# Local attention and an FFN in one kernel: seven wide chunks in place of twelve narrow ones, and a longer attention lead

## The chip, the cores and the metric

The kernel runs on one core of one Trainium2 chip. The metric is the time on the device in microseconds, from start to end of one execution; below are three runs and one profiled execution of the kernel before. A core has five engines with a queue each, worked off in order: TensorE (PE; its weight loads are PEld), VectorE (DVE), ScalarE (ACT), GpSimd (POOL) and SyncE (SP), which here only issues DMAs.

## The reference

```python
def _attn_ref(q, k, v, n_global, n_local):         # q, k, v: 4 batches, 8 heads, 768 tokens, 64 dims
    scores = scale * np.matmul(q, k.transpose(0, 1, 3, 2))
    is_global = pos[None, :] < int(n_global)       # 8
    is_local = (rel >= 0) & (rel < int(n_local))   # 96; rel = query position - key position
    dist = np.where(is_global & ~is_local, float(n_local), np.abs(rel))
    scores = np.where(is_global | is_local, scores - slopes * dist, -1e9)
    a = np.exp(scores - np.max(scores, axis=-1, keepdims=True))
    a = a / (np.sum(a, axis=-1, keepdims=True) + 1e-09)
    return np.matmul(a, v)

def _moe_ref(x, w_in, w_out):                      # 3072 x 512, 512 x 2048, 2048 x 512
    h = x @ w_in
    return np.maximum(0.01 * h, h) @ w_out
```

The attention's output, laid out as 3072 tokens by 512, is the FFN's input. The weights come in as float64, the rest as float32.

## The kernel before

**Attention.** A step is a block of 128 queries of one batch (24 steps), and each step has four units of two heads. A query block needs at most two blocks of keys, its own and one that holds the 32 first keys and the 96 before the block; the first step of a batch needs its own alone. `scores` multiplies queries by keys, VectorE adds the bias and takes the row minimum (line 199), ScalarE the exponential (209). `normalise` follows one unit later, `transposes` two, `attn_v` three. Units of the first batch (24, "plain") use float32 products, of two instructions each; the other 72 ("split") use pairs of rounded parts. The first eight units ("lead") run before the FFN. In these, `normalise` makes a diagonal matrix of the row factors on VectorE (line 223), and a float32 product with it transposes and scales in one (242); in all others Pool scales the probabilities (225) and TensorE transposes them (244). In the first six units, two products that nothing reads follow the transposes (`warm`, line 232).

**Weights.** 32 pieces of 512 KB of float64 bits, 16 for each matrix, in the order in which hidden tiles need them. `load_piece` brings one into a buffer of the pool `big` (ten buffers for several uses), and is called for piece p + 2 once piece p's conversion has been written down. `split_float64` converts with one step on ScalarE (436), three on VectorE (437, 439, 441), a rounding on Pool or ScalarE and a subtraction on Pool (449). Six pieces are converted during the lead.

**FFN.** A chunk is 256 tokens, twelve in all. A slot is one hidden tile of 128 units for one chunk: `hidden` makes twelve products into one PSUM tile (lines 639 to 641: 4 blocks of the input by 3 pairs of rounded parts), and four steps on ScalarE and VectorE apply the activation and split the result (643 to 648); `project` adds three products per token block of 128 to the chunk's output sums (655 to 657), one slot later. The first three chunks take the first ten hidden tiles in turn and then the other six, so their output sums are left once in the tile `part` and added to later (366, 369). Attention units and pieces of weights are dealt out evenly over slots. A scheduler orders the instructions of all this on each engine; the queues run them in that order. PSUM has eight banks: six in `ps_x` for hidden tiles, scores, transposes and values in rotation, and two in `ps_o` for output sums.

## Time and profile before

| | |
|---|---|
| runs, us | 738.5, 738.68, 744.76 (median 738.68) |
| span of the profiled execution | 743.0 us, 14545 instructions |
| busy share of the span | PE 97%, PEld 86%, DVE 69%, ACT 56%, POOL 43% |
| DMA | 47.69 MB, 64 GB/s over the span |
| chain that ended last | PE 82%, DVE 11%, issue 2%, DMA 2% |

Of the three runs, the profiled execution's span fits the longest only: 744.76 us holds a span of 743.0 us, the other two are shorter than it. A row of the timeline gives start, duration, engine, line, operation, what is written and read, shapes and a count. A matmul's duration includes its way through the array, so that products overlap in it; what one costs in a stream is read from the difference of two starts. A row of a group gives busy time and mean duration in ns, and then the engine's idle time before the group, with what ended it. In `64*128 64x256`, 64 is the number of rows of the array, 128 that of its columns, and 256 the columns that stream through.

### The profile page before, as it was taken

Reading aid. Unit: us, or ns where it says so; the run is one execution under the profiler, and the core shown is the slowest. Engines: PE = TensorE matmul, PEld = TensorE weight load, DVE = VectorE, ACT = ScalarE, POOL = GpSimd, SP = SyncE. Lnnn points to the kernel's source line nnn. Section 1 sums busy time; section 2 is a strip of 40 time slices with the busy share of each in tenths; the row PEclk is TensorE's granted clock in tenths of the full one; section 3 lists DMA queues with packets and bytes.
Section 4 is the critical chain, followed back from the end, with each engine's and each line's share of the span. In section 5 each row is a group of like instructions: output and inputs, shape, how many; then the busy total and the mean of one; then the engine's idle time right before and its main releaser. Section 6 shows DMA issues by size and latency. Waiting matters only on the chain.

```text
span 743.0 us, 14545 instructions
## 1 busy us (share of the span) xinstructions
PE 718.6 (97%) x4691; PEld 638.3 (86%) x4691; DVE 515.8 (69%) x1536; ACT 412.7 (56%) x1228; POOL 316.1 (43%) x563
## 2 busy tenths in 40 slices
PE   8979889999999999999999999999999999999995
PEld 7657667788999999999899999999999999999994
DVE  7699999764578877765777677776767776653222
ACT  4545667543566556654666665565656665643321
POOL 3389775831234444445344344445344544300000
PEclk9998999999999999999999999999999999999998
DMA  6454525130012111211211211211101211000000
GB/s 173 148 219 165 166 72 163 58 115 1 22 64 72 57 45 43 71 30 50 69 40 33 69 44 30 72 44 55 61 30 43 72 37 37 33 1 1 29 1 33
DMA packets 38916, 47.69 MB, mean 64 GB/s; under 512 B 5552, under 2 KB 27056, under 8 KB 38832
## 3 DMA queue, kind: packets, MB, share of 16 engines
q1 hardware_dynamic: 38832, 46.69, 20.1%
q8 instruction: 39, 0.64, 0.4%
q14 instruction: 45, 0.37, 0.2%
HBM read 40.37 MB, written 6.29 MB: 63 GB/s over the span
## 4 chain that ended last, share of the span: by engine, by line
PE 82%; DVE 11%; issue 2%; DMA 2%; ACT 1%; POOL 1%; SPq 0%; POOLq 0%; ACTq 0%; DVEq 0%
PE ps_h L641 11%; PE ps_h L640 11%; PE ps_h L639 11%; PE ps_o L655 11%; PE ps_o L656 11%; PE ps_o L657 11%; PE ps_av L287 4%; PE ps_tr L244 4%; DVE w L439 3%; PE ps_sc L191 2%; DVE w L441 2%; PE ps_sc L190 2%; PE ps_sc L188 2%; DVE w L437 1%; DVE gl L648 1%
## 5 line engine op out<-in xcount | busy, mean ns | idle before, releaser
L639 PE MATMUL ps_h<-xh,wih 128*128 128x256 f32 x768 | 219.7, 287 | 0.3 <-DVE xl L280 0.3
L640 PE MATMUL ps_h<-xl,wih 128*128 128x256 f32 x768 | 216.9, 283 | 1.9 <-DVE xl L280 1.9
L641 PE MATMUL ps_h<-xh,wil 128*128 128x256 f32 x768 | 217.1, 283 | 0.9 <-POOL wil L449 0.9
L655 PE MATMUL ps_o<-woh,gh 128*128 128x512 f32 x384 | 158.2, 412 | 1.2 <-ACT gh L647 1.2
L656 PE MATMUL ps_o<-wol,gh 128*128 128x512 f32 x384 | 153.3, 399 | 0.0
L639 PEld LDWEIGHTS ps_h<-xh,wih 128*128 128x128 f32 x768 | 145.9, 190 | 8.3 <-issue 1.2
L640 PEld LDWEIGHTS ps_h<-xl,wih 128*128 128x128 f32 x768 | 146.1, 190 | 7.8 <-DVE xl L280 2.1
L641 PEld LDWEIGHTS ps_h<-xh,wil 128*128 128x128 f32 x768 | 145.9, 190 | 6.9 <-POOL wil L449 1.6
L657 PE MATMUL ps_o<-woh,gl 128*128 128x512 f32 x384 | 142.1, 397 | 5.5 <-DVE gl L648 5.5
L225 POOL TENSOR_SCALAR pr<-pr,rs 128x256 f32<-128x256 f32 (+1 forms) x176 | 97.6, 564 | 106.5 <-DVE rs L218 88.4
L643 ACT ACTIVATE t<-ps_h 128x256 f32<-128x256 f32 x192 | 72.9, 380 | 102.3 <-PE ps_h L641 98.0
L648 DVE TENSOR_TENSOR gl<-t,gh 128x256 fp32r<-128x256 f32 x192 | 89.0, 464 | 52.3 <-ACT gh L647 50.5
L647 ACT CAST gh<-t 128x256 fp32r<-128x256 f32 x192 | 77.2, 402 | 74.7 <-DVE t L644 62.0
L644 DVE TENSOR_TENSOR t<-ps_h,t 128x256 f32<-128x256 f32 x192 | 80.6, 420 | 48.9 <-ACT t L643 46.6
L209 ACT ACTIVATE pr<-pr,nmall 128x256 f32<-128x256 f32 (+1 forms) x192 | 94.0, 490 | 19.2 <-DVE nmall L199 16.9
L55 POOL TENSOR_SCALAR qh<-qkr 128x256 fp32r<-128x256 f32 x72 | 29.9, 416 | 148.5 <-PE ps_sc L190 147.5
L657 PEld LDWEIGHTS ps_o<-woh,gl 128*128 128x128 f32 x384 | 70.0, 189 | 23.1 <-DVE gl L648 7.0
L655 PEld LDWEIGHTS ps_o<-woh,gh 128*128 128x128 f32 x384 | 73.0, 190 | 11.9 <-ACT gh L647 2.1
L656 PEld LDWEIGHTS ps_o<-wol,gh 128*128 128x128 f32 x384 | 72.9, 190 | 8.0
L199 DVE CUSTOM_DVE_ANT_0 pr<-ps_sc,nbw 128x256 f32<-128x256 f32 x96 | 38.9, 418 | 32.3 <-PE ps_sc L191 25.9
L165 ACT CAST kw<-qkr 64x256 fp32r<-64x256 f32 x72 | 29.2, 406 | 55.8 <-DMA qkr<-in_qk_dram 55.6
L166 DVE TENSOR_TENSOR kw<-qkr,kw 64x256 fp32r<-64x256 f32 x72 | 34.2, 476 | 34.4 <-ACT kw L165 33.7
(94 smaller groups left out, 1155.5 us busy)
## 6 DMA issues: line engine op xcount, KB each, us to landing
qkr<-in_qk_dram SPq DMA_DIRECT2D x72, 128.0 KB, 2.5
wst<-in_wi_dram SPq DMA_DIRECT2D x16, 512.0 KB, 4.3
wst<-in_wo_dram SPq DMA_DIRECT2D x16, 512.0 KB, 4.6
vr<-in_vp_dram SPq DMA_DIRECT2D x96, 64.0 KB, 1.9
out_dram<-part SPq DMA_DIRECT2D x24, 256.0 KB, 2.1
qkr<-in_qk_dram SPq DMA_DIRECT2D x72, 64.0 KB, 2.3
kr<-in_qk_dram SPq DMA_DIRECT2D x24, 64.0 KB, 2.6
qr<-in_qk_dram SPq DMA_DIRECT2D x16, 64.0 KB, 2.6
```

The costliest lines, as they stand in the source:

```text
L209: nc.scalar.activation(out=pr[:, j, :n], in_=pr[:, j, :n], func=AF.Exp, scale=-1.0, bias=nm[:, j:j + 1], accum_out=sm[:, j:j + 1])
L225: nc.gpsimd.tensor_scalar(out=pr[:, j, :n], in0=pr[:, j, :n], scalar1=rs[:, j:j + 1], scalar2=1.0, op0=ALU.mult, op1=ALU.mult)
L639: nc.tensor.matmul(ps, lhsT=wih[:, k, fs], rhs=xh[:, k, :], start=(k == 0), stop=False)
L640: nc.tensor.matmul(ps, lhsT=wih[:, k, fs], rhs=xl[:, k, :], start=False, stop=False)
L641: nc.tensor.matmul(ps, lhsT=wil[:, k, fs], rhs=xh[:, k, :], start=False, stop=(k == NK - 1))
L643: nc.scalar.activation(out=t, in_=ps, func=AF.Copy, scale=0.01)
L644: nc.vector.tensor_tensor(out=t, in0=ps, in1=t, op=ALU.max)
L647: nc.scalar.copy(out=gh, in_=t)
L648: nc.vector.tensor_tensor(out=gl, in0=t, in1=gh.bitcast(F32), op=ALU.subtract)
L655: nc.tensor.matmul(o, lhsT=gh[:, ts_], rhs=woh[:, f, :], start=first, stop=False)
L656: nc.tensor.matmul(o, lhsT=gh[:, ts_], rhs=wol[:, f, :], start=False, stop=False)
L657: nc.tensor.matmul(o, lhsT=gl[:, ts_], rhs=woh[:, f, :], start=False, stop=last)
```

## The change

- The FFN has seven chunks of 4, 2, 3, 4, 4, 4 and 3 steps (256 to 512 tokens), each through all 16 hidden tiles, so that there are no partial sums. `ps_o` has four banks and `ps_x` four. A chunk's attention units are dealt out over the first 14 slots of the chunk before.
- The lead has 16 units (four steps). All plain units transpose as the others do, after Pool has scaled the probabilities; the diagonal products and the products that nothing reads are gone, but for five at the very start.
- A plain unit's two heads lie in two halves of the partitions (arrays `qp` and `kp`), so that its two score products stand in different rows of the array and go to two PSUM tiles, of `ps_o` in the lead.
- The pool `big` is gone. Weight pieces have two buffers, which the output tiles take over later; the converted words share three with parts of attention; a chunk's inputs have two pairs.
- Six pieces are converted in the lead, after its steps 5, 7, ... 15, and the other 26 in the first 13 slots, two in each.

On TensorE, in the lead. Names: `ps_sc` scores, `ps_tr` transposes, `ps_av` values, `pr` probabilities, `kr_n` keys of one unit of a step. Before, where scores with two key blocks begin:

```order
L188 MATMUL ps_sc<-kr_112,qs 128x256 x2
L232 MATMUL ps_o<-pr,ident 128x128 x2
L242 MATMUL ps_tr<-diag,pr 128x128
L276 MATMUL ps_av<-ptp,vr_122 64x128 x2
L188 MATMUL ps_sc<-kr_116,qs 128x256 x2
L242 MATMUL ps_tr<-diag,pr 128x128
L232 MATMUL ps_o<-pr,ident 128x128 x2
L242 MATMUL ps_tr<-diag,pr 128x128 x4
```

After, in the same stage (line 172 is scores, 221 transposes, 252 values):

```order
L172 MATMUL ps_sc<-kr_115,qs 128x256 x2
L172 MATMUL ps_sc<-kr_119,qs 128x256 x2
L221 MATMUL ps_tr<-ident,pr 128x128 x4
L252 MATMUL ps_av<-ptb,vr_130 64x128 x2
L221 MATMUL ps_tr<-ident,pr 128x128 x4
L172 MATMUL ps_sc<-kr_107,qs 128x256 x2
```

The products of line 232 between scores and transposes are gone, and the transposes read the identity in place of a diagonal.

On ScalarE, in the first chunk, where it also rounds the weights. `w32` is a piece under conversion, read from its raw buffer `wst`; `t` and `gh` belong to a slot's activation; `wih` and `woh` are converted weights. Before:

```order
L436 ACTIVATE w32_874<-wst_803 128x512
L643 ACTIVATE t_911<-ps_h_898 128x256
L647 CAST gh_914<-t_911 128x256
L209 ACTIVATE pr_921,sm_922<-pr_921,nmall_71 128x256
L279 CAST xh_697<-ps_av_933 128x128
L209 ACTIVATE pr_921,sm_922<-pr_921,nmall_71 128x256
L250 COPY ptp_946<-ps_tr_941 128x512
L436 ACTIVATE w32_883<-wst_812 128x512
L446 CAST wih_72<-w32_874 128x4x128
```

After (404 is the first step of a conversion, 414 the rounding, 611 and 615 `t` and `gh`):

```order
L414 CAST woh_74<-w32_1093 128x512
L404 ACTIVATE w32_1166<-wst_1091 128x512
L227 COPY ptp_1162<-ps_tr_1157 128x512
L404 ACTIVATE w32_1175<-wst_1100 128x512
L414 CAST wih_72<-w32_1166 128x4x128
L611 ACTIVATE t_1209<-ps_h_1196 128x512
L196 ACTIVATE pr_1223,sm_1224<-pr_1223,nmall_71 128x256
L615 CAST gh_1212<-t_1209 128x512
L414 CAST woh_74<-w32_1175 128x512
```

Two first steps now stand in each slot with one other instruction between them, ahead of the slot's hidden tile, which is twice as wide.

```diff
-GROUP = 3           # chunks that share the parts of the weights at the start
-CUT = 10            # hidden tiles in the first part
-LEAD_PIECES = 6     # weight pieces converted before the first chunk, after these steps:
-LEAD_STEPS = [4, 5, 6, 7, 8, 9]
-WARM_UNITS = 6      # units during which products that nothing reads keep TensorE's clock up
+CHUNKS = [4, 2, 3, 4, 4, 4, 3]
+LEAD_CONV = {5: [0], 7: [1], 9: [2], 11: [3], 13: [4], 15: [5]}
...
-    big = ctx.enter_context(tc.tile_pool(name="big", bufs=10))
+    xts = ctx.enter_context(tc.tile_pool(name="xts", bufs=4))
-    ps_x = ctx.enter_context(tc.tile_pool(name="ps_x", bufs=6, space=bass.MemoryType.PSUM))
-    ps_o = ctx.enter_context(tc.tile_pool(name="ps_o", bufs=2, space=bass.MemoryType.PSUM))
+    ps_x = ctx.enter_context(tc.tile_pool(name="ps_x", bufs=4, space=bass.MemoryType.PSUM))
+    ps_o = ctx.enter_context(tc.tile_pool(name="ps_o", bufs=4, space=bass.MemoryType.PSUM))
...
-            t = big_tile([P, NK * P], I64, "wst")
+            t = raw.tile([P, NK * P], I64, tag="stage", name="wst")
...
-    LEAD = NU * SPC     # units of the first chunk, done before the FFN
+    LEAD = NU * CHUNKS[0]
...
+            if u < LEAD:
+                ps = [ps_o.tile([P, 2 * P], F32, tag="ps_o", name="ps_sc") for _ in range(2)]
             else:
+                ps = [ps_x.tile([P, 2 * P], F32, tag="ps_h", name="ps_sc") for _ in range(2)]
+            for j in range(2):
+                rows = slice(j * D, (j + 1) * D)
+                nc.tensor.matmul(ps[j][:, :n], lhsT=d["q"][rows, :], rhs=k[rows, keys], start=True, stop=True)
...
-        if u < LEAD:
-            d["diag"] = att.tile([P, 2, P], F32, tag="qh", name="diag")
         for j in range(2):
-            if u < LEAD:
-                nc.vector.tensor_scalar(out=d["diag"][:, j], in0=ident, scalar1=rs[:, j:j + 1], scalar2=None, op0=ALU.mult)
-            else:
-                nc.gpsimd.tensor_scalar(out=pr[:, j, :n], in0=pr[:, j, :n], scalar1=rs[:, j:j + 1], scalar2=1.0,
-                                        op0=ALU.mult, op1=ALU.mult)
+            nc.gpsimd.tensor_scalar(out=pr[:, j, :n], in0=pr[:, j, :n], scalar1=rs[:, j:j + 1], scalar2=1.0,
+                                    op0=ALU.mult, op1=ALU.mult)
...
-        if u < WARM_UNITS:
-            warm(d["pr"][:, 0, :P], 2)
...
-    order = ffn_order(NCHUNK, NF)
+    order = [(c, f) for c in range(NCHUNK) for f in range(NF)]
...
+        for tt in range(CHUNKS[c]):
+            ob = raw.tile([P, DM], F32, tag="stage", name="part")
+            if tt % 2:
+                nc.vector.tensor_copy(out=ob, in_=o[tt])
+            else:
+                nc.scalar.copy(out=ob, in_=o[tt])
+            r0 = (first_step[c] + tt) * P
+            nc.sync.dma_start(out=out[r0:r0 + P, :], in_=ob)
...
+    for c in range(1, NCHUNK):
+        t0, t1 = NU * first_step[c] + A_LAG, NU * first_step[c + 1] + A_LAG
+        events += [lambda t=t: unit_step(t) for t in range(t0, t1)]
+        add(units_at, spread(events, range((c - 1) * NF, c * NF - 2)))
+        events = []
+    lead_conv = sum(len(x) for x in LEAD_CONV.values())
+    add(conv_at, spread(range(lead_conv, 2 * NF), range(0, NF - lead_conv // 2)))
```

170 lines of the change are left out of this document (69 added, 101 removed).

## The prediction

> **What bounds the kernel now.** I read the busy time by stretch first, because one average over the span would mix three stages with different limits. The cuts are my own: 39 us is where the FFN begins, 137 us where VectorE stops being full, 734 us where the last product starts.
>
> ```profile
> core 0: us, PE busy (x) PEld busy (x) DVE busy (x) ACT busy (x) POOL busy (x), PEclk, DMA share, GB/s
> 0.00:39.00 39.00, 34.58 (x163) 27.03 (x164) 27.32 (x104) 19.40 (x60) 15.55 (x33) 1.00 0.57 167
> 39.00:137.00 98.00, 87.09 (x511) 64.69 (x510) 96.21 (x212) 59.78 (x164) 77.62 (x96) 0.95 0.44 146
> 137.00:734.00 597.00, 596.39 (x4017) 546.42 (x4018) 391.57 (x1222) 332.90 (x1004) 222.94 (x436) 1.00 0.14 44
> 734.00:743.00 9.00, 0.59 (x3) 0.16 (x1) 0.69 (x1) 0.58 (x1) 0.00 (x0) 0.67 0.19 67
> ```
>
> The rows add up to the span of 743.0 us. For 597 us TensorE is busy to within 0.6 us: there only the number and the pace of its products count. From 39 to 137 us VectorE is full (96.21 of 98) with the conversion of the weights. The first 39 us belong to the attention units ahead of the FFN, and the last 9 to the end. A busy TensorE says nothing of its pace, so next I read starts in the timeline, first in the middle of the long stage.
>
> ```profile
> 399.85 0.39 PE L656 MATMUL ps_o<-wol,gh 128*128 128x512 f32 x1
> ...
> 401.01 0.28 PE L639 MATMUL ps_h<-xh,wih 128*128 128x256 f32 x1
> ...
> 403.05 0.40 PE L655 MATMUL ps_o<-woh,gh 128*128 128x512 f32 x1
> ...
> 405.29 0.28 PE L190 MATMUL ps_sc<-kw,qh 128*128 128x256 f32 x1
> ...
> 406.59 0.48 PE L655 MATMUL ps_o<-woh,gh 128*128 128x512 f32 x1
> 406.91 0.39 PE L656 MATMUL ps_o<-wol,gh 128*128 128x512 f32 x1
> ```
>
> Five products of 512 columns start between the first two rows: 1.16 / 5 = 0.232 us each. Seventeen of 256 columns start between the second and the third: 2.04 / 17 = 0.120 us. So two of 256 cost 0.240 and one of 512 costs 0.232: a wider product saves 3%, not more. One split unit of attention (scores, values, transposes) runs from 405.29 to 406.59, and the product after its transposes is late by 0.09 (0.32 instead of 0.232): 1.39 us. For a unit with one key block I take 0.75, an estimate: half its score and value products are there.
>
> The timeline of TensorE in the first stage shows another pace.
>
> ```profile
> 19.42 2.07 PE L188 MATMUL ps_sc<-kr,qs 64*128 64x256 f32 x4
> 21.42 1.22 PE L232 MATMUL ps_o<-pr,ident 128*128 128x128 f32 x4
> 22.43 0.63 PE L242 MATMUL ps_tr<-diag,pr 128*128 128x128 f32 x2
> ...
> 28.91 0.70 PE L276 MATMUL ps_av<-ptb,vr 128*64 128x128 f32 x4
> 29.54 1.58 PE L188 MATMUL ps_sc<-kr,qs 64*128 64x256 f32 x4
> ...
> 38.78 0.39 PE L639 MATMUL ps_h<-xh,wih 128*128 128x256 f32 x1
> ...
> 41.11 1.13 PE L188 MATMUL ps_sc<-kr,qr 64*128 64x256 f32 x4
> 42.17 0.62 PE L639 MATMUL ps_h<-xh,wih 128*128 128x256 f32 x3
> ```
>
> The same four score instructions take 2.00 us at 19.42 and 1.06 us at 41.11. The clock column reads 1.00 in both, so I go by the durations: TensorE runs at half speed until about 29.5 us, although it has hardly a gap. The Trainium skill ("TensorE: Matmul & The Clock Gate", Part 1) has full rate follow about 3.4 us of sustained activity; this trace disagrees, with some 20 us of dense work at half rate. The same page (Part 4) says that transposes do not count as activity for the clock in the same way.
>
> **The change, part by part.** I sum the stages and compare with the span of 743.0 us. Of the three runs shown only the longest, 744.76, can hold such a span; their median, 738.68, lies 4.3 below it. The difference to 743.0 is carried over to the median.
>
> *FFN products.* Columns and weights stay; only the grouping changes. A slot (one hidden tile of one chunk) has 12 products into the hidden tile and three per token block out of it. At 256 tokens: 12 x 0.120 + 6 x 0.232 = 2.83 us; at 512: 24 x 0.232 = 5.57; at 384, with 0.176 for the width between: 12 x 0.176 + 9 x 0.232 = 4.20. Before: 192 slots of 2.83 = 543.7. After: 64 x 5.57 + 32 x 4.20 + 16 x 2.83 = 536.1, so 7.6 us less.
>
> *Chunks 1 to 6.* All but chunk 0's 89.1 us of that, 447.0, and the 72 split units, 60 x 1.39 + 12 x 0.75 = 92.4: 539.4 us. Before, TensorE waited 0.6 us in such a stage. Now PSUM gives four banks instead of six to everything but the output sums, and at a chunk's end four sums leave through two buffers, so that the third copy waits on its engine for the first output DMA, with that slot's activation steps queued behind it. The next chunk needs those banks only after its first hidden products (2.8 us), so I take 1 us at each of six ends; the bounds are 0 and 2. Stage: 545.4. VectorE does more per slot in the narrow chunk 1, where twelve units share 14 slots, but 391.57 busy of 597 leaves room. The partial sums removed (copies and additions) lie beside full TensorE work: nothing.
>
> *The lead.* Eight more units come before the FFN, each with two key blocks. At half speed one costs: scores 2.00 us, values 2 x 0.63 = 1.26, four transposes at most the 0.92 us of four products like L242 (0.23 each) and no less than 0.35 at full speed; I take 0.75, near the slow end, since the stage is slow. The scores now lie in two halves of the array's rows. Each float32 product is two instructions; if starts keep their order, the second half can run beside the first half's second instruction only, which hides one of four: 0.43 us. Nothing in this trace runs two row halves at once, so the bounds are 0 and 1.0. Unit: 1.57 + 0.75 + 1.26 = 3.6 us (bounds 2.6 and 4.2). The Trainium skill ("TensorE: Matmul & The Clock Gate", Part 3) has row tiles run fully side by side; with that the unit would be 3.0 and the lead 5 us shorter.
>
> The 24 clock-keeping instructions go, four of which take 1.01 us: 6 us less. The products with a diagonal become transposes: 2 us less (0 to 5). Lead: 38.8 + 8 x 3.6 - 6 - 2 = 59.6; without the clock-keeping products the FFN probably starts at half speed, 2 us more: 62. In place of VectorE's diagonal, Pool now scales every lead unit. These are Pool's rows from 39 to 137 us, where it shares its time with VectorE:
>
> ```profile
> L225 POOL TENSOR_SCALAR pr<-pr,rs 128x256 f32<-128x256 f32 x30 | 21.4, 723 | 9.0 <-DVE rs L218 8.8
> L449 POOL TENSOR_TENSOR wil<-w,wih 128x512 fp32r<-128x512 f32 x13 | 17.6, 1356 | 2.3 <-ACT wih L446 2.2
> L449 POOL TENSOR_TENSOR wol<-w,woh 128x512 fp32r<-128x512 f32 x12 | 16.7, 1390 | 1.6 <-ACT woh L446 1.5
> L55 POOL TENSOR_SCALAR vr<-vr 32x128 f32<-32x128 f32 x13 | 7.0, 538 | 1.2 <-PE ps_av L276 1.2
> L55 POOL TENSOR_SCALAR kr<-kr 64x64 f32<-64x64 f32 x12 | 5.9, 491 | 0.5 <-DMA kr<-in_qk_dram 0.5
> ```
>
> Twelve units of 2 x 0.723 + 0.538 + 0.491 = 2.5 us, four of about 0.8 and six conversions of about 2.0: 45 us. Pool stays just short of TensorE; had TensorE full speed, Pool would end the lead at 50 to 55. Without overlap and with slow transposes it is 38.8 + 8 x 4.2 - 6 + 2 = 68. Lead: 50 to 68.
>
> *Chunk 0.* TensorE has 16 x 5.57 = 89.1 us and eight plain units of 1.06 + 0.44 + 0.70 = 2.2 (the warm scores above, a split unit's transposes, values at half of 1.26 with a tile switch): 107. Beside it 26 weight pieces are converted, two per slot in 13 slots. A piece's buffer now is one of two instead of one of ten, so load, first step and VectorE's three steps follow one another:
>
> ```profile
> L441 DVE SCALAR_TENSOR_TENSOR w<-wst,w 128x512 int32<-128x512 int32 x24 | 25.3, 1059 | 0.1
> L439 DVE SCALAR_TENSOR_TENSOR w<-wst,w 128x512 int32<-128x512 int32 x24 | 22.7, 950 | 0.0
> L437 DVE TENSOR_SCALAR w<-w 128x512 int32<-128x512 int32 x23 | 15.3, 665 | 0.3 <-ACT w L436 0.3
> L648 DVE TENSOR_TENSOR gl<-t,gh 128x256 fp32r<-128x256 f32 x15 | 11.1, 748 | 0.9 <-ACT gh L647 0.9
> ```
>
> ```profile
> DMA to landing us min/median/max: 3.4/4.5/7.1
> ```
>
> ```profile
> L436 ACT ACTIVATE w<-wst 128x512 f32<-128x512 f32 x22 | 14.8, 678 | 11.1 <-POOL wol L449 4.7 <-POOL wil L449 4.6 <-DMA wst<-in_wo_dram 1.6
> ```
>
> One turn: 4.5 + 0.68 + 0.67 + 0.95 + 1.06 = 7.9 us, with a semaphore or two 8.0; each buffer turns once per slot. A slot's own TensorE work is 5.57 + 8/13 x 2.2 = 6.9, so the loop is the longer. While ScalarE waits for a landing, the evacuation of the hidden tile and the rounding of the activation stand behind it in its queue, and TensorE waits for those; SP's queue holds the next units' loads behind a refused weight load in the same way. So 13 x 8.0 = 104 and 3.2 slots after the last conversion, 18: 122. Bounds: 107, if hidden, and 139, if 1.3 us of waiting in line joins each turn (the turn is then 9.3).
>
> *End.* Nine us as before; three outputs now leave through two buffers, and the third waits for the first DMA.
>
> ```profile
> out_dram<-part SPq DMA_DIRECT2D x24, 256.0 KB, 2.1
> ```
>
> The first sum is complete some 1.4 us before the last (six products of 0.232), which leaves 0.7 of the 2.1 us, and its copy before the DMA adds an estimated half: 10.2.
>
> Sum: 62 + 122 + 545.4 + 10.2 = 739.6, 3.4 us under 743.0; against the median, **735.3**, 0.5% less.
>
> **The rivals.** *Slower: the staging loop is the clock of chunk 0.* At 9.3 us a turn chunk 0 takes 139, the total is 17 us more, 752 on the median. For it: ScalarE's order after the change puts two first steps almost next to each other and the hidden tile behind them, and there were 11.1 us of waits before such steps already with ten buffers. Against it: loads land in 3.4 us when few are under way. It decides from a turn of 8.8 us: 13 x 0.8 = 10.4 us more is 746.
>
> *Faster: TensorE's clock rises early in the lead.* Two row halves at once fill the array, which the present scores do not. Pool then ends the lead near 52 us, ten less: 725. For it: at 29.5 us the clock did rise, just after a run of full-array products. Against: transposes and half-array products are most of what is left, and the clock-keeping products are gone. It decides from a lead that ends before 58. The rule of Part 1 cited above would have this happen. With the loop hidden as well it is 710.
>
> *No overlap of the row halves*, so that this part does not do what it says: the lead is 12 x 0.43 + 4 x 0.21 = 6 us longer, 741: still no change.
>
> **How the numbers follow.** About 1%, 7.4 us, is what a measurement of this kernel can tell from no change. My forecast lies within it: 0.38, the third rival included. The faster rival gets 0.36, since half the lead's price rests on the half speed and 18 us lie between its bounds; the slower one 0.26. The forecast's own range is 729 to 744. With the two rivals, 8 in 10 reach from 719 to 754; beyond it lie the cases in which two bounds meet on one side.
>
> **What would show it.** The first 512-wide product at 55 to 66 us confirms the lead; its four score instructions near 1.6 us confirm the partial overlap, 1.0 the full one, 2.0 none. Weight conversions 4.0 us apart with ScalarE waiting for a weight landing confirm the loop; 3.5 us apart with TensorE full refutes it. From chunk 1 on TensorE should wait for less than 8 us in all. The forecast is wrong if TensorE shows gaps through the middle chunks (four banks too few), or if chunk 0 falls below half speed again, as the clock of 0.95 in the second stretch shows can happen.

## The result, and the profile after

The changed kernel takes 745.54 us, median of 20 (742.48 to 748.93); the kernel before has a median of 740.83 us over 20 (737.14 to 748.3). The ratio is 1.0053, with a 95% interval of 1.0028 to 1.0078: half a per cent slower. The forecast was 735.3 us, half a per cent faster. The profiled execution after the change spans 744.3 us.

The busy time by stretch after the change. The cuts are the first FFN product (57.3), the first copy of chunk 0's sums out of PSUM (184.8) and the first copy of the last chunk's (734.2); the columns are those of the same view of before.

```profile
0.00:57.30 57.30, 46.42 (x242) 27.89 (x242) 39.04 (x147) 32.99 (x107) 39.40 (x84) 0.76 0.48 147
57.30:184.80 127.50, 118.29 (x564) 88.47 (x563) 99.08 (x211) 66.70 (x158) 80.64 (x98) 0.97 0.38 122
184.80:734.20 549.40, 543.17 (x2879) 468.22 (x2878) 357.84 (x1007) 280.92 (x792) 209.97 (x397) 1.00 0.13 41
734.20:744.30 10.10, 0.46 (x2) 0.02 (x1) 0.69 (x1) 1.17 (x2) 0.00 (x0) 0.63 0.24 87
```

The third row differs from the long stage of before: TensorE is idle for 6.2 us of it, where it was idle for 0.6 of 597. To see the whole loss I count TensorE's products that start between the two copies and price them as the prediction did. There are 168 hidden products of 256 columns, 384 of 384 and 576 of 512, and 961 output products; the units have 236 scores of 256 columns (0.12 us each), 32 of 128 (0.10), 260 values (0.1175) and 260 transposes (0.11). That is 20.16 + 67.58 + 133.63 + 222.95 + 90.67 = 535.0 us. The stage takes 549.4, so **14.4 us are lost after chunk 0**. Of these, 6.2 are the idle time; 1.7 are a stretch of 3.4 us at half clock, shown in the last section; the rest are products that start late while the one before them still counts as busy (one of 512 columns counts for 0.4 us, the next can start after 0.232). The same count is used for every kernel below.

The four chunks inside that stage, in the same view (chunks 2, 3, 4 and 5, from first copy to first copy):

```profile
246.10:339.00 92.90, 90.57 (x513) 82.15 (x512) 73.57 (x221) 56.25 (x170) 50.46 (x98) 0.98 0.18 52
339.00:453.70 114.70, 112.52 (x575) 94.00 (x574) 79.84 (x225) 62.14 (x175) 52.45 (x96) 1.00 0.15 45
453.70:565.90 112.20, 110.92 (x561) 92.34 (x560) 75.47 (x221) 60.14 (x175) 50.55 (x96) 1.00 0.16 48
565.90:668.90 103.00, 103.00 (x505) 86.17 (x504) 57.06 (x149) 43.91 (x110) 23.93 (x46) 1.00 0.08 25
```

Their products come to 87.7, 110.6, 109.0 and 102.4 us, so the chunks lose 5.2, 4.1, 3.2 and 0.6. Chunk 1 loses 1.2 and chunk 6 0.1. Chunks 2 to 4 have 16 units dealt over 14 slots; chunk 1 and chunk 5 have 12, chunk 6 none. What TensorE waited for in the stage, by the view of waits (us, times, longest):

```profile
PE ps_o L623 <- ACT gh L615: 3.0, 4, 1.5
PE ps_h L607 <- DVE nmall L186: 2.2, 4, 0.6
PE ps_av L263 <- DVE pt L232: 0.7, 2, 0.4
```

One of these waits, step by step, in the timeline of chunk 3 (start, duration, engine, line, in brackets the idle time before it and what ended it):

```profile
416.96 0.73 POOL L142 TENSOR_TENSOR qhl<-qkr,qhl 128x256 fp32r<-128x256 f32 x1
...
417.72 0.47 SPq L123 DMA_DIRECT2D qkr<-in_qk_dram  x1
...
420.36 0.41 ACT L144 CAST kw<-qkr 64x256 fp32r<-64x256 f32 x1 [2.50 <-DMA qkr<-in_qk_dram]
...
420.67 0.59 ACT L611 ACTIVATE t<-ps_h 128x512 f32<-128x512 f32 x1
420.80 0.42 DVE L145 TENSOR_TENSOR kw<-qkr,kw 64x256 fp32r<-64x256 f32 x1 [2.41 <-ACT kw L144]
...
421.25 0.42 DVE L186 CUSTOM_DVE_ANT_0 pr<-ps_sc,nbw 128x256 f32<-128x256 f32 x1
...
421.94 0.69 DVE L612 TENSOR_TENSOR t<-ps_h,t 128x512 f32<-128x512 f32 x1
...
422.17 0.47 PE L607 MATMUL ps_h<-xh,wih 128*128 128x512 f32 x1 [0.64 <-DVE nmall L186]
```

Pool frees the buffer of a load only at 417.69, so the keys are loaded late. ScalarE stands still for them for 2.50 us with the evacuation of the hidden tile queued behind, VectorE for 2.41 us with the reading of the scores queued behind, and TensorE gets its next PSUM bank when VectorE has read them. The transfer is the last cause named here; the experiments ask whether it is the cause.

The lead and the start of the FFN, in the timeline of TensorE:

```profile
13.12 2.08 PE L172 MATMUL ps_sc<-kr,qs 64*128 64x256 f32 x8
...
16.98 1.14 PE L172 MATMUL ps_sc<-kr,qs 64*128 64x256 f32 x8
...
58.76 0.63 PE L607 MATMUL ps_h<-xh,wih 128*128 128x512 f32 x1
59.19 0.63 PE L608 MATMUL ps_h<-xl,wih 128*128 128x512 f32 x1
...
61.41 0.40 PE L608 MATMUL ps_h<-xl,wih 128*128 128x512 f32 x1
61.64 0.40 PE L609 MATMUL ps_h<-xh,wil 128*128 128x512 f32 x1
```

Eight score instructions, two units, take the time that four took before, 2.0 us at half speed and 1.1 at full: the two row halves overlap completely. The FFN starts with products 0.43 us apart and reaches 0.23 after some 3.6 us.

Most times of the kernel before fall into two groups (736.6 to 740.3 and 743.9 to 748.8 us in the 19 of one comparison; of the 20 above, 741.71 and 743.2 lie between), and its profiled execution, 744.76 us, lies in the upper one; the granted clock of the two groups is the same, 0.99.

### The profile page after: what moved, and what is told of

Its sections match the earlier page's. It is cut to its first block, busy times and chain, and to the rows that moved or that the text cites. A ratio compares the mean times of both kernels' runs of the same rounds, so it can differ in the third digit from the quotient of the medians.

```text
span 744.3 us, 12086 instructions
## 1 busy us (share of the span) xinstructions
PE 708.3 (95%) x3683; PEld 584.6 (79%) x3683; DVE 496.6 (67%) x1364; ACT 381.8 (51%) x1058; POOL 330.0 (44%) x579
## 4 chain that ended last, share of the span: by engine, by line
PE 58%; DVE 13%; DMA 9%; POOL 7%; ACT 6%; issue 5%; POOLq 0%; ACTq 0%; DVEq 0%; SPq 0%
PE ps_h L607 8%; PE ps_o L623 8%; PE ps_h L608 8%; PE ps_h L609 8%; PE ps_o L624 8%; PE ps_o L625 7%; DMA qkr<-in_qk_dram 7%; PE ps_tr L221 3%; ACT pr L196 3%; PE ps_av L263 2%; DVE pr L186 2%; PE ps_sc L172 2%; POOL qhl L142 2%; POOL pr L207 2%; PE ps_av L252 1%
## 5 line engine op out<-in xcount | busy, mean ns | idle before, releaser
L607 PE MATMUL ps_h<-xh,wih 128*128 128x512 f32 (+2 forms) x448 | 167.3, 374 | 5.4 <-DVE nmall L186 5.2
L609 PE MATMUL ps_h<-xh,wil 128*128 128x512 f32 (+2 forms) x448 | 163.4, 365 | 1.5 <-POOL wil L417 1.5
L608 PE MATMUL ps_h<-xl,wih 128*128 128x512 f32 (+2 forms) x448 | 163.7, 366 | 0.0
L207 POOL TENSOR_SCALAR pr<-pr,rs 128x256 f32<-128x256 f32 (+1 forms) x192 | 113.1, 597 | 109.0 <-ACT gh L615 42.0
L612 DVE TENSOR_TENSOR t<-ps_h,t 128x512 f32<-128x512 f32 (+2 forms) x112 | 68.3, 610 | 64.7 <-ACT t L611 64.2
L607 PEld LDWEIGHTS ps_h<-xh,wih 128*128 128x128 f32 x448 | 84.9, 190 | 21.4 <-issue 3.6
L609 PEld LDWEIGHTS ps_h<-xh,wil 128*128 128x128 f32 x448 | 85.1, 190 | 14.5 <-POOL wil L417 1.9
L608 PEld LDWEIGHTS ps_h<-xl,wih 128*128 128x128 f32 x448 | 85.2, 190 | 11.2
L616 DVE TENSOR_TENSOR gl<-t,gh 128x512 fp32r<-128x512 f32 (+2 forms) x112 | 70.1, 626 | 21.8 <-ACT gh L615 20.7
L615 ACT CAST gh<-t 128x512 fp32r<-128x512 f32 (+2 forms) x112 | 62.1, 554 | 28.1 <-DVE t L612 25.7
L221 PE MATMUL ps_tr<-ident,pr 128*128 128x128 f32 x352 | 61.3, 292 | 3.7 <-POOL pr L207 3.3
```

Source lines behind the costliest of these rows:

```text
L207: nc.gpsimd.tensor_scalar(out=pr[:, j, :n], in0=pr[:, j, :n], scalar1=rs[:, j:j + 1], scalar2=1.0, op0=ALU.mult, op1=ALU.mult)
L221: nc.tensor.transpose(out=pt_ps[:, j, c, :], in_=d["pr"][:, j, c * P:(c + 1) * P], identity=ident)
L607: nc.tensor.matmul(ps, lhsT=wih[:, k, fs], rhs=xh[:, k, :CT], start=(k == 0), stop=False)
L608: nc.tensor.matmul(ps, lhsT=wih[:, k, fs], rhs=xl[:, k, :CT], start=False, stop=False)
L609: nc.tensor.matmul(ps, lhsT=wil[:, k, fs], rhs=xh[:, k, :CT], start=False, stop=(k == NK - 1))
L612: nc.vector.tensor_tensor(out=t, in0=ps, in1=t, op=ALU.max)
```

## The experiments

Sixteen kernels ran. The theories are named in the expectations: **A**, the four PSUM banks make TensorE wait in the middle chunks; **B**, units that stand two to a slot; **D**, the density of units; **Q**, late loads of keys; **U**, that no slot is left without a unit, so that nothing late is caught up; and for chunk 0 **E**, the conversion loop. "Lost" is the time after chunk 0 over its counted products, as above. The count is good to about 1 us: products of 384 columns start 0.174 to 0.177 us apart, and in eight chunks some 1320 of them are counted. "Chunk 0" runs to the first copy of its sums; where two kernels with the same chunks differ in their products after it, the difference was done ahead of the cut in one of them and is a part of its chunk 0.

| kernel | ratio to before (95%) | FFN starts | chunk 0 | after chunk 0 | its products | lost |
|---|---|---|---|---|---|---|
| changed | 1.0053 (1.0028 to 1.0078) | 57.3 | 127.5 | 549.4 | 535.0 | 14.4 |
| changed, second execution | 1.0079 (1.0043 to 1.0114) | 55.4 | 126.4 | 549.2 | 534.8 | 14.4 |
| units over 16 slots | 0.9953 (0.9919 to 0.9986) | 58.4 | 120.4 | 548.9 | 537.2 | 11.7 |
| six chunks of 512, 16 slots | 1.0104 (1.0056 to 1.0152) | 55.4 | 141.5 | 535.4 | 526.5 | 8.9 |
| 512, six of 384, 256, 16 slots | 0.9874 (0.9828 to 0.9919) | 58.5 | 126.0 | 538.9 | 535.8 | 3.1 |
| eight of 384, five banks, 16 slots | 0.9877 (0.9835 to 0.9919) | 46.8 | 114.5 | 558.3 | 557.2 | 1.1 |
| eight of 384, four banks, 16 slots | 0.9915 (0.9878 to 0.9951) | 47.2 | 116.9 | 559.0 | 558.1 | 0.9 |
| the same, units over 12 slots | 1.0123 (1.0085 to 1.0161) | 47.1 | 127.4 | 564.8 | 556.9 | 7.9 |
| the same, third load buffer | 1.0092 (1.0060 to 1.0124) | 47.1 | 128.3 | 563.5 | 556.6 | 6.9 |
| 12 slots, five banks | 1.0073 (1.0043 to 1.0103) | 46.8 | 127.0 | 560.7 | 556.4 | 4.3 |

**Four banks alone**

```diff
-    ps_x = ctx.enter_context(tc.tile_pool(name="ps_x", bufs=6, space=bass.MemoryType.PSUM))
+    ps_x = ctx.enter_context(tc.tile_pool(name="ps_x", bufs=4, space=bass.MemoryType.PSUM))
```

> The kernel before with four PSUM banks instead of six for everything but the output sums, and nothing else changed. Theory A (four banks are what makes TensorE wait in the middle chunks after the change): the stage from 137 us to the last product, which waited 0.6 us with six banks, gets 8 to 14 us of waits, a ratio to the kernel before of 1.010 to 1.019. Rival B (the waits come from units that are issued two to a slot, or from the chains of 512-wide steps, not from the number of banks): that stage keeps under 2 us of waits and the ratio is 0.997 to 1.003.

Measured: 747.91 us, ratio 1.0105 (1.0043 to 1.0167). The ratio is A's, but not the place. The long stage of this kernel, in the view by stretch:

```profile
137.00:734.00 597.00, 596.31 (x4016) 546.58 (x4016) 388.92 (x1213) 331.79 (x1004) 221.46 (x434) 1.00 0.14 44
```

TensorE is idle for 0.7 us of 597, as with six banks. Whatever four banks cost, they cost it before 137 us, beside the conversions; the profile shows only 2.1 us of it there (the last product starts at 736.3 instead of 734.2), and these six times scatter over 10 us. Theory A is refuted for the middle chunks at the rate of units that the kernel before has (one in every second slot); why four banks cost 1% in all stays open.

**The row halves alone, and with the transposes.** The first of the two kernels changes only the layout of the first batch's queries and keys and the scores in the kernel before; the second also replaces the diagonal.

```diff
+            ps = [ps_x.tile([P, 2 * P], F32, tag="ps_h", name="ps_sc") for _ in range(2)]
+                rows = slice(j * D, (j + 1) * D)
+                nc.tensor.matmul(ps[j][:, :n], lhsT=d["q"][rows, :], rhs=k[rows, keys], start=True, stop=True)
...
-                    nc.tensor.matmul(pt_ps[:, j, c, :], lhsT=src, rhs=d["diag"][:, j], start=True, stop=True)
+                nc.tensor.transpose(out=pt_ps[:, j, c, :], in_=src, identity=ident)
```

> The kernel before with the first batch's scores in two halves of the array's rows, and nothing else of the change: same chunks, same partial sums, same products with a diagonal, same clock-keeping products. If TensorE sets the length of the lead, the eight lead units save 4 x 0.5 + 4 x 1.0 = 6 us at half speed: FFN starts at 33 instead of 39 us, ratio 0.990 to 0.994. If the lead waits for other engines or for loads, it starts at 37 to 39 us, ratio 0.997 to 1.001. From 39 to 137 us VectorE is full, so the scores saved there give nothing in either case.

> The kernel before with the scores in two row halves, and in the eight lead units plain transposes after Pool has scaled the probabilities, instead of products with a diagonal that VectorE makes; clock-keeping products kept. In the kernel with the row halves alone TensorE waits 4.7 us for that diagonal in the lead. If VectorE's diagonal holds the lead, the FFN starts at 31 to 33 us instead of 35.9, ratio to the kernel before 0.988 to 0.993. If Pool's scaling (0.7 us a head, two a unit) takes its place as the last, it starts at 35 to 39 us, ratio 0.994 to 1.000.

Measured: 737.42 us, ratio 0.9950 (0.9921 to 0.9978) for the row halves, and 738.38 us, 0.9963 (0.9933 to 0.9993) with the transposes. The first FFN product in the timeline and TensorE's longest wait in the lead, for the row halves alone:

```profile
35.89 0.58 PE L638 MATMUL ps_h<-xh,wih 128*128 128x256 f32 x1
```

```profile
PE ps_tr L241 <- DVE diag L222: 4.7, 2, 3.4
```

With the transposes too, the same two, and the stretch from the start of the FFN to 137 us:

```profile
33.14 0.58 PE L630 MATMUL ps_h<-xh,wih 128*128 128x256 f32 x1
```

```profile
PE ps_tr L235 <- POOL pr L219: 6.9, 4, 4.0
```

```profile
33.00:137.00 104.00, 91.27 (x567) 67.88 (x567) 98.06 (x225) 61.97 (x174) 85.30 (x107) 0.94 0.43 141
```

The row halves bring the FFN forward by 2.9 us, half of the 6 that TensorE's own work promised, since it then waits for VectorE's diagonal; the transposes bring it forward by another 2.8, now with waits for Pool's scaling. The second gain is worth nothing: VectorE is busy for 98.06 of the next 104 us, and both kernels' last sums are ready within 0.3 us of each other. A lead that ends earlier does not help where the stage behind it is full on another engine. Not all of the 0.5% of the row halves is their work either: their twelve times (736.5 to 738.2 us) hold none of the upper group of the kernel before, and against the lower group alone (15 of its 29 times here, median 738.65) the gain is 1.2 us.

**The deal over 16 slots**

```diff
-        add(units_at, spread(events, range((c - 1) * NF, c * NF - 2)))
+        add(units_at, spread(events, range((c - 1) * NF, c * NF)))
```

> The changed kernel with the attention units of a chunk dealt over 16 slots of the chunk before instead of 14, so that no slot holds two units of a 512-wide chunk. Theory B1 (units issued two to a slot make TensorE wait): of the 9 us of TensorE waits that stand in the profile of the changed kernel between 175 and 660 us some 6 go, ratio to the kernel before 0.995 to 0.999 where the changed kernel has 1.005. Theory A (four banks) and the theory that a chunk's output makes the waits: 1.003 to 1.008, as the changed kernel; if the last unit is late for the next chunk, a wait of 2 to 4 us at each of six chunk starts, 1.015 to 1.03.

Measured: 739.84 us, ratio 0.9953 (0.9919 to 0.9986). The gain is as large as B1 said and lies elsewhere:

```profile
58.40:178.80 120.40, 114.04 (x546) 85.56 (x545) 98.70 (x200) 63.92 (x151) 79.40 (x95) 0.98 0.40 127
178.80:727.70 548.90, 542.55 (x2897) 468.81 (x2896) 358.04 (x1019) 280.75 (x801) 215.76 (x400) 1.00 0.14 42
```

Chunk 0 takes 120.4 us instead of 127.5, and 2.2 of these 7.1 us are products that here stand behind the cut. The stage behind it loses 11.7 instead of 14.4; 1.7 of this difference is the stretch of half clock, which this kernel does not have there. Two units in one slot are a small part of the middle's loss; beside the conversions a tight deal costs more, 4.9 us.

**Clock-keeping products in the lead**

```diff
+        if u < LEAD:
+            warm(2)
```

> The changed kernel with two clock-keeping products after the transposes of each of the 16 lead units, as the first six lead units had them before. If the half clock sets the length of the lead, the granted clock in the first 57 us rises from 0.77 to above 0.9, the FFN starts at 52 to 55 us and runs at full speed at once: ratio 0.995 to 1.000 where the changed kernel has 1.005. If the lead is held by Pool and the loads, the added products cost 0 to 8 us: FFN start 57 to 64 us, ratio 1.003 to 1.014.

Measured: 745.06 us, ratio 1.0053 (1.0022 to 1.0084). The first 55 us of the changed kernel and of this one:

```profile
0.00:55.00 55.00, 44.85 (x233) 27.04 (x234) 38.28 (x144) 31.61 (x105) 37.64 (x82) 0.78 0.47 143
```

```profile
0.00:55.00 55.00, 45.80 (x310) 32.03 (x311) 38.77 (x146) 33.17 (x108) 37.62 (x83) 0.97 0.48 147
```

The clock rises as expected and the FFN starts at 54.1 at full speed, 3.2 us earlier than in the first execution and 1.3 earlier than in the second; the time does not change. Against the second execution the first copy of chunk 0's sums comes 0.4 us earlier (181.4 instead of 181.8), and the stage behind it takes 551.2 us instead of 549.2, so the chunks behind the lead take back what the start gained; to what they lose it, this run does not show.

**One VectorE step of the conversion left out**

```diff
-    nc.vector.scalar_tensor_tensor(out=wb, in0=lo, scalar=29, in1=wb,
-                                   op0=ALU.logical_shift_right, op1=ALU.bitwise_or)
```

> The changed kernel with one of VectorE's three steps in each weight conversion left out (the one that takes in the low word's three bits, 1.06 us); the weights lose their last bits, and nothing else changes. Theory E (the staging loop of 8 us a slot sets chunk 0): a turn falls to 6.9 us, which is TensorE's own work in the slot, chunk 0 falls from 117.6 to 103 to 108 us, ratio to the kernel before 0.985 to 0.992 where the changed kernel has 1.005. Rival (loads, or chains of the units, set chunk 0): under 4 us, ratio 1.000 to 1.005.

Measured: 730.62 us, ratio 0.9861 (0.9814 to 0.9908), 15 us under the changed kernel; the profiled execution, 737.74 us, is the longest of the six. Chunk 0 in the view by stretch:

```profile
60.20:173.90 113.70, 112.06 (x546) 84.00 (x545) 80.40 (x178) 64.34 (x153) 77.08 (x96) 1.00 0.45 139
```

It takes 113.7 instead of 127.5 us (2.2 of the 13.8 are products that here stand behind the cut) and TensorE is busy for 112.06 of them, so that this chunk has become TensorE's. The loss behind it is as large as before (14.8). So the conversions do set chunk 0; whether by the loop through two buffers or by VectorE's work, this kernel cannot say, since it shortens both.

**A third buffer for the weight pieces.** In chunks of 512 there is no room for it; eight chunks of 384 have it.

```diff
-            t = raw.tile([P, NK * P], I64, tag="stage", name="wst")
+            t = raw.tile([P, NK * P], I64, tag="stage", name="wst", bufs=3)
...
-        load_piece(p + 2)
+        load_piece(p + 3)
```

> The kernel with eight chunks of 384 tokens and five banks, even deal, with a third buffer for the weight pieces, so that a piece is loaded three conversions ahead instead of two. Theory E1 (the loop of load, ScalarE and VectorE through two buffers sets chunk 0): VectorE's 9.5 us of waits for ScalarE's first step go, chunk 0 gets 8 to 12 us shorter, ratio to the kernel before 0.972 to 0.979 where two buffers have 0.988. Rival E2 (VectorE's work itself sets it): 0 to 3 us, ratio 0.984 to 0.989.

Measured: 733.06 us, ratio 0.9887 (0.9850 to 0.9923), where two buffers have 0.9877. Chunk 0 in the view by stretch and VectorE's wait for the first step in the view of waits (up to 140 us), with two buffers and then with three:

```profile
46.80:161.30 114.50, 105.70 (x579) 83.02 (x578) 100.29 (x226) 67.15 (x170) 84.63 (x106) 0.97 0.44 141
```

```profile
DVE w L405 <- ACT w L404: 9.5, 11, 1.9
```

```profile
48.70:160.80 112.10, 102.44 (x566) 78.85 (x565) 100.04 (x224) 64.93 (x170) 88.50 (x107) 0.99 0.43 140
```

```profile
DVE w L406 <- ACT w L405: 3.8, 5, 1.7
```

The waits shrink from 9.5 to 3.8 us. Chunk 0 is 2.4 us shorter, but 2.1 us of products have moved behind its cut, so next to nothing is gained. VectorE is busy for 100 us of it with either. That is E2 in this kernel: VectorE's work sets chunk 0, not the loop. For chunks of 512, where VectorE is busy for 99.08 of 127.5 us, it is not shown.

**Six chunks of 512**, with the deal over 16 slots.

```diff
-CHUNKS = [4, 2, 3, 4, 4, 4, 3]
+CHUNKS = [4, 4, 4, 4, 4, 4]
```

> The changed kernel with six chunks of 512 tokens, units dealt over 16 slots. There is no narrow chunk any more, so a unit comes every 7.0 us in chunks 1 to 4 (in the changed kernel every 5.4 us in chunk 1, every 5.7 us in chunk 2); chunk 0 has 16 units beside the conversions instead of 8. Theory D (density: waits grow with the units per microsecond): from the end of chunk 0 on TensorE loses 3 to 4 us per chunk over its products, 14 in all, as chunks 3 and 4 of the changed kernel do. Rival (the narrow chunks make the waits): under 6 us in all. In both cases chunk 0 grows by 10 to 20 us with eight split units beside the conversions: total 745 to 755, ratio 1.006 to 1.02.

Measured: 746.77 us, ratio 1.0104 (1.0056 to 1.0152). Chunk 0 with 16 units takes 141.5 us, as expected in both cases. Behind it 8.9 us are lost, between the two expectations (14 and under 6): narrow chunks are not needed for the loss, and wide ones do not bring as much as chunks 3 and 4 suggested. This run decides nothing.

**Eight chunks of 384, with five banks and with four**, with the deal over 16 slots. The diff is that of five banks; four banks leave `ps_x` as it is.

```diff
-CHUNKS = [4, 2, 3, 4, 4, 4, 3]
+CHUNKS = [3, 3, 3, 3, 3, 3, 3, 3]
...
-    ps_x = ctx.enter_context(tc.tile_pool(name="ps_x", bufs=4, space=bass.MemoryType.PSUM))
-    ps_o = ctx.enter_context(tc.tile_pool(name="ps_o", bufs=4, space=bass.MemoryType.PSUM))
+    ps_x = ctx.enter_context(tc.tile_pool(name="ps_x", bufs=5, space=bass.MemoryType.PSUM))
+    ps_o = ctx.enter_context(tc.tile_pool(name="ps_o", bufs=3, space=bass.MemoryType.PSUM))
```

> The changed kernel with eight chunks of 384 tokens, three PSUM banks for output sums and five for the rest, 12 lead units, units dealt over 16 slots. Sum: lead 46, chunk 0 118 (conversion loop), seven chunks of 67.2 and units for 92.4, end 10: 737, plus the waits of the middle. Theory A (number of banks): with a fifth bank under 4 us of waits after chunk 0, 737 to 741, ratio 0.996 to 1.001. Rival (VectorE's and ScalarE's queues make the waits, whatever the banks): 10 to 14 us, 747 to 751, ratio 1.009 to 1.014.

> As the kernel with eight chunks of 384 tokens and five banks, with four banks for everything but the output sums (one bank of PSUM unused). Theory A: 8 to 12 us slower than with five. Rival (queues of VectorE and ScalarE): within 2 us of it.

Measured: 731.13 us, ratio 0.9877 (0.9835 to 0.9919) with five, and 734.70 us, 0.9915 (0.9878 to 0.9951) with four. The stage behind chunk 0, five banks and four:

```profile
161.30:719.60 558.30, 557.92 (x3122) 512.08 (x3121) 367.14 (x1050) 296.39 (x839) 218.72 (x406) 1.00 0.14 42
```

```profile
164.10:723.10 559.00, 558.45 (x3128) 512.75 (x3127) 365.14 (x1047) 296.50 (x836) 217.92 (x405) 1.00 0.14 41
```

TensorE is idle for 0.4 and 0.6 us. The number of banks makes no difference there, and with four banks the wait of the changed kernel is gone, although units come as often, 12 in a chunk of some 83 us, as in its chunks 3 and 4, 16 in 112 to 115. What differs, besides the width, is that 12 units over 16 slots leave every fourth slot without one. The two kernels are 3.6 us apart, more than the 2 of the rival and far less than the 8 of A; 2.4 of it is chunk 0's (114.5 and 116.9). For the whole time both expectations were too long: their sum before any wait, 737, is 6 us over the measured 731.13, 3.5 of it in chunk 0 (118 against 114.5). With five banks this kernel is faster than the one before and the changed one.

**The same chunks with a unit in every slot.** The second of the three kernels has `bufs=3` for the loads of queries and keys and `load_qk(t + 4)` in place of `load_qk(t + 3)`, the third five banks in `ps_x`.

```diff
-        add(units_at, spread(events, range((c - 1) * NF, c * NF)))
+        add(units_at, spread(events, range((c - 1) * NF, c * NF - 4)))
```

> The kernel with eight chunks of 384 tokens and four banks, units dealt over 12 of the 16 slots of a chunk: where there are units, one comes every 4.20 + 1.39 = 5.6 us, as in chunk 2 of the changed kernel. Theory D (density): TensorE loses about 0.3 us per unit, as in that chunk (5.6 us for 16 units), 72 x 0.3 = 22 us after chunk 0; at the least 8 us. Ratio to the kernel before 1.00 to 1.02, where the even deal has 0.992. Rival (it is the 512-wide steps of VectorE and ScalarE that make the waits): under 2 us, ratio 0.989 to 0.995.

> The same dense deal with a third buffer for the loads of queries and keys, each issued one unit earlier. Theory Q (the wait begins with ScalarE's first step on a late load of keys; the evacuation of the hidden tile stands behind it): of what the dense deal costs after chunk 0 more than two thirds goes, ratio within 0.3% of the even deal's 0.992. Rival (Pool and VectorE are full at this density, whenever the load lands): less than a third goes.

> The same dense deal with five banks instead of four. Theory A (banks): the fifth bank takes away more than half of what the dense deal costs after chunk 0. Rival (queues of the other engines): less than a quarter.

Measured: 751.20 us, ratio 1.0123 (1.0085 to 1.0161) for the dense deal; 748.52 us, 1.0092 (1.0060 to 1.0124) with the third load buffer; 747.25 us, 1.0073 (1.0043 to 1.0103) with five banks. The stage behind chunk 0 of the dense deal, and ScalarE's wait for the keys between 200 and 655 us:

```profile
174.50:739.30 564.80, 560.78 (x3118) 511.62 (x3118) 363.06 (x1038) 293.25 (x830) 208.57 (x397) 1.00 0.13 41
```

```profile
ACT kw L144 <- DMA qkr<-in_qk_dram: 39.6, 58, 2.2
```

With the third buffer for the loads, the same two:

```profile
175.40:738.90 563.50, 559.85 (x3118) 511.48 (x3117) 363.08 (x1037) 293.84 (x828) 211.93 (x397) 1.00 0.13 40
```

```profile
ACT kw L144 <- DMA qkr<-in_qk_dram: 22.4, 41, 2.0
```

The dense deal loses 7.9 us in the stage where the even one loses 0.9: as little as D allowed (8) and far from its 22. Chunk 0 grows by another 10.5 (127.4 instead of 116.9), 1.2 of them products done ahead of the cut. Earlier loads take ScalarE's wait for the keys from 39.6 to 22.4 us and give back 1.0 of the 7.0 us: theory Q is refuted as the main cause, though the timeline above names such a load. The fifth bank gives back 3.8 of 7.0 (from 0.9 to 7.9 with four banks, from 1.1 to 4.3 with five). That is about half, too near to the bound of theory A to decide for it by a count good to 1 us; but banks have a large share once every slot has a unit.

**The first chunk kept, the rest thinned**, with the deal over 16 slots.

```diff
-CHUNKS = [4, 2, 3, 4, 4, 4, 3]
+CHUNKS = [4, 3, 3, 3, 3, 3, 3, 2]
```

> The changed kernel with chunks of 512, six times 384 and 256 tokens, units dealt over 16 slots: lead, first chunk, four banks and two buffers as in the changed kernel, but behind chunk 0 no slot in four consecutive ones is without a free one (12 units in 16 slots; in the changed kernel chunks 2, 3 and 4 have 16 in 16). Theory U (units per slot: with one unit in every slot a late step of VectorE is never caught up): after chunk 0 TensorE loses under 3 us over its products instead of 12 to 16. Products 537.6 instead of 536.1, chunk 0 with four more units 0 to 8 us longer than their products: 739.8 (the even deal's time) + 1.5 - 10 + 0 to 8 = 731 to 739, ratio 0.987 to 0.997. Rival (the 14 us belong to the wide first chunk, its buffers or the boundaries): 8 us or more are still lost after chunk 0, ratio 0.999 to 1.01.

Measured: 733.23 us, ratio 0.9874 (0.9828 to 0.9919). The stage behind chunk 0:

```profile
184.50:723.40 538.90, 537.65 (x3069) 492.61 (x3067) 349.98 (x1014) 283.70 (x809) 206.06 (x388) 1.00 0.14 42
```

With the lead, the first chunk, the four banks and the two buffers of the changed kernel, 3.1 us are lost instead of 11.7, where U asked for under 3 and its rival for 8 or more. That speaks for U. The width of the chunks changed with the deal, though: no run has chunks of 512 with every fourth slot free. The nearest is chunk 5 of the changed kernel, 512 wide with 12 units in 14 slots, which loses 0.6 us. By the ratios the thinned kernel is 0.8% faster than the even deal of the changed chunks.

**Second executions of both kernels**

> The kernel before, unchanged, for a second profiled execution. The first lies 3.9 us above the median of 20 times. If the half clock of its first 137 us made that (two stretches, 6.8 and 3.4 us long, behind the first 30 us), an execution near the median shows less of it, and its last product starts 2 to 5 us before the 734.2 us of the first; from 137 us on both have under 1 us of TensorE waits. If it is something in the long stage, the same stage is 2 to 5 us shorter instead. Ratio 0.997 to 1.003.

> The changed kernel, unchanged, for a second profiled execution. If the waits of the middle chunks belong to the order of the work, the time from the first copy of chunk 0's sums to the first copy of the last chunk's is again 548 to 551 us (549.4 in the first), with chunks 2, 3 and 4 within 1 us of 92.9, 114.7 and 112.2. If they are chance, they lie elsewhere or the stage is over 3 us off. The lead, whose clock changes between full and half, may differ by 5 us. Ratio 1.003 to 1.008.

Measured: the kernel before 743.87 us, ratio 1.0013 (0.9973 to 1.0053); the changed kernel 745.74 us, 1.0079 (1.0043 to 1.0114). The long stage of the first, and the stage behind chunk 0 with chunks 2, 3 and 4 of the second:

```profile
137.00:734.00 597.00, 596.19 (x4016) 546.30 (x4017) 392.39 (x1222) 332.73 (x1005) 222.86 (x436) 1.00 0.14 44
```

```profile
181.80:731.00 549.20, 543.07 (x2879) 468.19 (x2878) 358.41 (x1007) 281.15 (x793) 210.47 (x397) 1.00 0.14 41
...
242.90:335.60 92.70, 90.65 (x513) 82.24 (x512) 73.58 (x221) 56.44 (x170) 50.59 (x98) 0.98 0.18 52
335.60:450.50 114.90, 112.41 (x575) 94.01 (x574) 79.96 (x225) 62.09 (x175) 52.62 (x96) 1.00 0.15 44
450.50:562.70 112.20, 110.99 (x561) 92.28 (x560) 75.84 (x222) 60.29 (x175) 50.76 (x96) 1.00 0.16 48
```

The middle repeats to 0.2 us: its waits belong to the order of the work. The lead moved by 1.9 us and chunk 0 by 1.1. The second execution of the kernel before, 745.43 us, fell into the upper group again and looks like the first, so where the two groups part is not shown; one of its two half-clock stretches is 3.4 us shorter than in the first, and its last product starts no earlier (734.4), so those stretches are not it.

## Why the prediction was wrong, step by step

By the cuts of the first table, with the products that TensorE does ahead of the cut moved from one term to the other (539.4 - 535.0 = 4.4 us), and with the cold start, which the forecast has in the lead and the cut in chunk 0: 3.7 us at half speed behind the first FFN product, 1.8 us longer than at full speed:

| term | forecast | measured | difference |
|---|---|---|---|
| lead, cold start included | 62 | 57.3 + 1.8 = 59.1 | -2.9 |
| chunk 0, to the first copy of its sums | 122 + 4.4 = 126.4 | 127.5 - 1.8 = 125.7 | -0.7 |
| behind it, six chunk ends at 1 us included | 545.4 - 4.4 = 541.0 | 549.4 | +8.4 |
| end | 10.2 | 10.1 | -0.1 |
| sum | 739.6 | 744.3 | +4.7 |

**The step that failed** is the price of waiting in chunks 1 to 6: "so I take 1 us at each of six ends". 14.4 us are lost there instead of 6, and not at the ends: the 10 us around each of the six ends (from 1 us before the first copy) lose 0.6 us together, chunks 1, 5 and 6 lose 1.9, chunks 2 to 4 lose 12.5. The prediction's own sign, under 8 us of waits from chunk 1 on, would not have told: idle time is 6.2 us, and the rest is lost without a gap in the view. The prediction weighed the banks ("four banks instead of six") and VectorE's mean load ("391.57 busy of 597 leaves room"). It did not count the units against the slots: before, 72 units had 139 slots; after, the 48 units of chunks 3 to 5 have 42, so a unit stands in every slot. Thinning to 12 units in 16 slots takes the loss to 3.1 us with the same four banks, and filling the slots of a kernel that loses 0.9 us takes it to 7.9, of which a fifth bank takes back about half. That the chain from Pool through ScalarE's and VectorE's queues then has no slot in which to catch up is argued from the timeline above, not shown by itself.

**The sign of the forecast** also hung on the execution profiled before. The miss of 10.2 us is 4.7 in the sum above; 3.4 because the profiled time of before (744.76) lies 3.9 above its median of 740.83 and that of after (746.07) 0.5 above 745.54; and 2.15 because the median of the three times shown (738.68) is that much under the median of 20. Had the profile stood at its median, the same sum would have read as about no change.

**The lead.** The cold start was right: products 0.43 us apart until about 61 us. The overlap of the row halves was wrong: "which hides one of four" is refuted by 1.1 us for two warm units. The Trainium skill ("TensorE: Matmul & The Clock Gate", Part 3) has row tiles run side by side, and these rows agree with it: 2.0 times for two halves. The price worked out by that rule, 5 us less, is 57 with the cold start, where 59.1 were measured; in other executions of the same lead the FFN started between 55.4 and 58.5, with other stretches of half clock. Pool was busy for 39.4 us, not 45; TensorE waited 3.3 us for its scaling in the lead, and 4.4 us for VectorE's reading of the scores.

**Chunk 0** came out within 0.7 us of the forecast by luck: two errors cancel. The forecast has the 26 conversions done after 104 us and 3.2 slots of TensorE's work behind them. The last conversion ended at 177.9 us, 120.6 after the first FFN product, and the first copy came 6.9 us later, so little of TensorE's work was left by then. First steps of conversions came 4.7 us apart (56.1 to 173.3 us), which makes a turn of 9.4 us for the two of a slot, not 8.0. The conversions do set the chunk: taking one VectorE step out shortens it by 11.6 us, without the products moved. Whether the loop of "4.5 + 0.68 + 0.67 + 0.95 + 1.06" through two buffers or VectorE's own work is the reason stays open here. By the prediction's sign the loop is at work: ScalarE waits 21.0 us for weight landings in chunk 0, in the view of waits (57.3 to 184.8 us):

```profile
ACT w L404 <- DMA wst<-in_wo_dram: 11.5, 8, 2.8
ACT w L404 <- DMA wst<-in_wi_dram: 9.5, 3, 4.7
```

With chunks of 384 it waits 16.0 us for them (46.8 to 150 us); there the third buffer leaves 3.4 of it, and next to nothing is gained. The loop's first term was too long in any case; the page of the profile after gives, in its list of transfers (the last number is the median time to landing):

```profile
wst<-in_wi_dram SPq DMA_DIRECT2D x16, 512.0 KB, 3.4
wst<-in_wo_dram SPq DMA_DIRECT2D x16, 512.0 KB, 3.5
```

With that the steps of a turn come to 6.9 us; the other 2.5 of the 9.4 are waits between them. VectorE is busy for 78% of this chunk in the changed kernel and 88% with chunks of 384, and the deal over 16 slots alone gives 4.9 us there. The prediction took the 11.1 us of waits before ScalarE's first steps in the kernel before as a sign for a slow turn; by the row that it shows, 9.3 of them ended with Pool and 1.6 with a landing.

**The rivals.** The slower rival had the right sign and the right turn (9.3 us against 9.4 measured), but chunk 0 did not reach its price of 139 us, since it too put 3.2 slots behind the last conversion, and the loss lies elsewhere. The faster one had set 58 us as the point from which the lead decides, and the FFN did start at 57.3, but not by its mechanism: the granted clock is 0.76 up to there, and the FFN starts at half speed. The row halves alone brought the FFN forward by 2.9 us; the middle took more than the whole lead gained. No overlap of the row halves is refuted. **The ends and the products** were priced right: 10.1 against 10.2 us, and where nothing waits (the kernels with eight chunks, 558.3 and 559.0 us) the counted products give 557.2 and 558.1.

What stays open: why four banks in the kernel before cost 1%, why the times of that kernel have two groups, how the loss at one unit a slot divides among VectorE, ScalarE and Pool, and what sets chunk 0 with chunks of 512. A third buffer for the weight pieces was not tried with chunks of 512 for lack of room, nor was a deal that leaves every fourth slot of such chunks free.

## What to carry to other kernels

When side work is dealt over the slots of a main loop, count the pieces per slot in each stage, not the mean load of the engines: at three pieces in four slots 1 to 3 us were lost here, at one in every slot 8 to 14 us with the same four banks, and VectorE was busy for some 70% of a chunk of 384 in both deals. A chain that ends in a wait on a transfer is not thereby a transfer problem; taking that wait from 39.6 to 22.4 us gave back a seventh of the loss. A term that comes out right is not thereby understood: chunk 0's did so by two errors of some 16 us each. Before a sum is made against one profiled execution, see where its time lies among the others: 5.5 of the 10.2 us of this miss were there.

## What the runs showed of the hardware

The clock fell to half after a wait of 1.5 us. Three successive stretches of the changed kernel around its longest wait in the middle:

```profile
286.00:289.60 3.60, 1.99 (x15) 1.63 (x14) 2.47 (x10) 2.36 (x9) 0.37 (x2) 1.00 0.25 73
289.60:293.10 3.50, 3.50 (x9) 2.76 (x10) 3.15 (x11) 1.75 (x7) 3.00 (x7) 0.51 0.07 19
293.10:296.60 3.50, 3.50 (x26) 3.46 (x25) 2.15 (x5) 1.83 (x5) 2.15 (x6) 1.00 0.25 75
```

TensorE idles for about 1.6 of 3.6 us, and for the next 3.4 us its products run 0.43 us apart although it is busy throughout, which costs another 1.7 us. It happened at the same wait in both executions. Behind chunk 0 of the changed kernel and its variants it followed a wait of 1.5 us or more in four executions (both of these, the one with clock-keeping products and the one with a step left out), and none of the shorter waits, of which the longest is 1.2 us (units over 16 slots). The Trainium skill ("TensorE: Matmul & The Clock Gate", Part 1) gives a window of 3413 ns, which this stretch fits, and has a whole idle window bring half rate; here a stretch a little over half busy did.

The two row halves of a float32 product, which is two instructions, overlap fully at either clock: 2.0 us for eight instructions at half speed, 1.1 at full.
